# Attention and a gated FFN on one core: all 896 tokens of batches 4 and 5 through Strassen units of 448 columns, and the attention's visits dealt out anew

## The chip, the core and the metric

The kernel runs on one core of a Trainium2 chip. The core has a matrix engine (TensorE, PE in the profile, with PEld for its weight loads), a vector engine (VectorE, DVE), a scalar engine (ScalarE, ACT), a general engine (GpSimd, POOL) and one that mostly issues transfers (SyncE, SP). Each engine works through its own queue of instructions in order and waits on semaphores for the others. Scores, products and sums of matmuls land in PSUM; everything else lies in SBUF.

The metric is the device time of one execution in microseconds. The times shown are medians of several runs; the profile is of one further execution, whose own time stands beside its span below. All stretches of time that are named in this document count from the first instruction of that profiled execution.

## What is computed

Eight batches of 448 tokens, twelve heads of 64. Attention without a mask gives x with 8 x 448 = 3584 rows of 768, and a gated FFN with 1536 hidden columns follows:

```python
scores = scale * (q @ k.transpose(0, 1, 3, 2))
attn = softmax(scores)
x = (attn @ v).transpose(0, 2, 1, 3).reshape(3584, 768)
g = x @ w_gate                      # 768 -> 1536
silu = g * (1.0 / (1.0 + exp(-g)))
out = (silu * (x @ w_val)) @ w_out  # 1536 -> 768
```

Inputs and output are fp32; the loads turn q, k, v and the weights to fp16, sums stay fp32.

## The kernel before

**Two streams on TensorE.** Heads are taken in pairs: 48 pairs, six for a batch. For a pair, TensorE makes the scores transposed (`qk`, `qk_quad`, rows of L356 and L368: keys on the partitions, queries along the columns), ScalarE takes the exponential of a chunk of both heads (L376, 128 x 896), TensorE multiplies by V with a column of ones for the row sums (`pv_mm`, L457), and VectorE divides (`pv_close`: a reciprocal L499 and a product L500 for each head) into `xt`. SP turns `xt` into X, the FFN's input with features on the partitions (`turn_x`, L545 and L551). The FFN works on X in blocks of tokens: two batches make 896 tokens (`kk` 0 to 3), cut into a block of 384 and one of 512 (`block`). Blocks are numbered 0 to 7; blocks 4 and 5 are the tokens of batches 4 and 5.

**A step** (`Step`) is one of the twelve slices of 128 hidden columns of a block: six matmuls for the gate (`gp`, `gate`), six for the value (`vp`, `value`), all L605. ScalarE takes a tanh of the gate (`sg`, L632), VectorE makes t = (sg + 1) gp (L660) and hts = t vp (L666), the hidden activations. A step can be cut: then the value goes in two halves of columns, the first into a spare half of the gate's PSUM tile and only the second into a buffer of its own.

**PSUM** is dealt out by two pools. `ps_s` has three tiles of two banks: each chunk of scores, each gate and the wide sums of a pair of output tiles take one. `ps_f` has two tiles of one bank: the two accumulators of P times V (one for a head), `vp` and the second sum of an output pair take them in turn. A tile is given out again when its readers are done.

**The second half of the FFN** (`w_out`) goes either plainly (`plain_out`, L700; twelve matmuls for 128 tokens and some output columns, called an output step here) or by Strassen's seven products for two tiles of 128 tokens at once (`OutPair.wide`, L724), whose sums of hidden activations VectorE makes (`h_sums`, L588 to L591).

**The first half by Strassen.** Batches 6 and 7 (`kk` = 3) and block 5 do not run as steps. Twelve units (`Unit`, L876), alternately gate and value, each treat two slices of hidden columns and two halves of the tokens at once by seven products of three matmuls, `w` columns wide: 448 for batches 6 and 7, 256 for block 5's 512 tokens. A unit needs four sums of weights (`weight_sums`, POOL, L839 to L842) and the stage needs four sums of tokens (`token_sums`, VectorE, L1059 to L1062). `order_of` orders a stage's instructions from estimated costs; it runs when the program is built. `run_wide` follows with the output pairs.

**What orders the attention.** An opening is written out by hand. After it, a plan deals out the chunks of scores, three at a time; each entry is a visit. In the program's order a visit has: its three chunks of scores, the first products of a P times V, its rest, and then what FFN work is put there. From plan entry 19 on this is read from the table VISITS, 33 entries, which I count from 0:

```python
begins, nf, ng, no, ns = VISITS[x - base]
```

`nf` is a number of steps (two run as `run_pair`, interleaved and the second cut; one as `run_single`, cut), `ng` of wide output pairs, `no` of output steps, `ns` of extra VectorE sums, and `begins` names a block whose predecessor's output work is queued. In every seventh visit (3, 10, 17, 24, 31) no P times V ends; the code calls them bare. `open_products` takes the two `ps_f` tiles of a P times V just before its first products, which go to the two heads in turn:

```python
pv_mm(pr, hx, RU, j, accs[pr][hx], j == 0, False, half if small else None)
```

The loads of q, k and v (POOL's queue, L180 and L203) run some pairs ahead; POOL copies q and k into the order that a transposing transfer needs (L240), and SP issues that transfer (`qkT`, L244). X has two buffers: batches 4 and 5 take over the one of batches 0 and 1, batches 6 and 7 the one of batches 2 and 3, whose steps must be through by then.

After the last visit come the units of block 5, with POOL's remaining weight sums, one output step, three output pairs (one of block 4, two of block 5), the units of batches 6 and 7 with a plain output of the 128 tokens left over, and three output pairs that end the kernel.

Of the kernel before, what the change touches and what calls it, by code (L numbers as in the profile page):

```python
# [17 lines left out]
NB = 2  # L18
# [5 lines left out]
RL = 4  # L24
# [41 lines left out]
def kernel(  # L66
# [898 lines left out]
    with tc.manual_schedule():  # L965
# [50 lines left out]
        def add_block(i, visits):  # L1016
            if i < B - NB - 1:
                f1, own, n = block(i)
                fvq.extend(f1)
                kk, c0, hts = own  # L1020
            else:
                own = None
# [12 lines left out]
            new = [OutPair(kk, c0, hts, t) for t in range(1 + odd)]  # L1035
# [74 lines left out]
        def run_single():  # L1110
            step = fvq.pop(0)
            step.split = step.alone = not gate_small[0]
            step.gate()
            step.value(0)
            step.finish()
            add_sum()
# [110 lines left out]
        hts5 = hview(384, 512)  # L1227
        vfree = vraw[:].rearrange("p s h c d -> p (s h c d)")
        VE = 2 * NC * D
        t5 = token_space(vfree[:, 3 * VE :], 256)  # L1230
        for x, (chunks, todo) in enumerate(plan):
# [43 lines left out]
            for _, p0 in todo:  # L1275
# [4 lines left out]
                if p0 < XPE:  # L1280
                    turns.append(p0)
                else:
# [26 lines left out]
            else:  # L1309
# [22 lines left out]
                if x == len(VISITS) + base - 6:  # L1332
                    space = raws_all[:, 0 : RL // 2].rearrange("p a t b x -> p (a t b x)")
                    wsum_space(space, 10)
# [3 lines left out]
                    wsum_space(vfree, 4)  # L1338
# [8 lines left out]
        x5 = X[KL - 1][:, :, 384:]  # L1347
# [50 lines left out]
        units = {}  # L1398
        items = unit_items(units, lambda u: Unit(u, 256, x5, t5, hts5), 256)
# [10 lines left out]
        for u in range(6, NFB):  # L1410
            items[f"W_{u}"] = (POOL_, 3.65, [f"W_{u - 1}"], lambda u=u: weight_sums(u))
        groups5 = [OutPair(KL - 1, 384, hts5, t, 1 - t) for t in range(2)]
        sums.clear()
        halves = [h_sums(hview(0, 384), 0, 0, nc.gpsimd, f0, NH // 2) for f0 in (0, NH // 2)]
        for m, fn in enumerate(fn for both in zip(*halves) for fn in both):
            items[f"G{m}"] = (POOL_, 0.95, [f"G{m - 1}" if m else f"W_{NFB - 1}"], fn)
        items["O"] = (PE_, 1.0, [f"P{n}_{NFB - 1}" for n in (2, 3, 7)], run_o)
        items[f"P4_{NFB - 1}"][2].append("O")
        run_items(items)

        def run_wide(pairs):
            for n, pair in enumerate(pairs):
                pair.wide(kept[2 * (n % 2) : 2 * (n % 2) + 2], add_sum)

        x7 = X[KL]
# [63 lines left out]
```

## Time and profile before

| what | value |
|---|---|
| median of 3 runs | 426.44 us (426.18 to 427.26) |
| the profiled execution | 426.04 us, span 424.3 us, granted TensorE clock 0.998 |
| matmuls | 4382 |
| visits 1 to 23 | 126.3 to 258.4 us |
| visits 24 to the end of the attention | 258.4 to 297.4 us |
| units of block 5, output step, three pairs | 297.4 to 347.3 us |
| units of batches 6 and 7 | 347.3 to 399.2 us |
| last three pairs and stores | 399.2 to 424.3 us |

Busy time of an engine in a stretch counts a matmul from its start to its modelled end, and matmuls overlap: "busy 99%" does not say that the next one started as early as it could. What TensorE's work takes is read from start to start in the timeline, where a row gives its start, the time to the end of its last instruction, engine, line, operation and how many instructions it merges; in brackets stands the idle time before it and who ended it.

### The profile page before, as it was taken

Reading aid. Unit: us, or ns where it says so; the run is one execution under the profiler, and the core shown is the slowest. Engines: PE = TensorE matmul, PEld = TensorE weight load, DVE = VectorE, ACT = ScalarE, POOL = GpSimd, SP = SyncE. Lnnn points to the kernel's source line nnn. Section 1 sums busy time; section 2 is a strip of 40 time slices with the busy share of each in tenths; the row PEclk is TensorE's granted clock in tenths of the full one; section 3 lists DMA queues with packets and bytes.
Section 4 is the critical chain, followed back from the end, with each engine's and each line's share of the span. In section 5 each row is a group of like instructions: output and inputs, shape, how many; then the busy total and the mean of one; then the engine's idle time right before and its main releaser. Section 6 shows DMA issues by size and latency. Waiting matters only on the chain.

```text
span 424.3 us, 10917 instructions
## 1 busy us (share of the span) xinstructions
PE 418.0 (99%) x4382; PEld 264.0 (62%) x4382; DVE 264.5 (62%) x610; ACT 243.6 (57%) x385; POOL 230.0 (54%) x351
## 2 busy tenths in 40 slices
PE   8999999999999999999999999999999999999996
PEld 3666666655556676656656766667888655555554
DVE  4767562776668564674645766577776655665662
ACT  6975667646755654655666547569655125555221
POOL 8656625997996766357448573965999000000000
PEclk9999999999999999999999999999999999999999
DMA  9999999999999999999999998831101240000124
GB/s 137 180 200 200 200 179 190 141 165 197 187 171 120 182 128 147 127 107 159 136 107 142 158 147 161 97 99 26 22 2 25 89 129 21 2 0 2 37 82 143
DMA packets 108307, 50.29 MB, mean 119 GB/s; under 512 B 60384, under 2 KB 105056, under 8 KB 108256
## 3 DMA queue, kind: packets, MB, share of 16 engines
q0 software_dynamic: 46800, 24.56, 49.2%
q1 hardware_dynamic: 61184, 24.79, 32.1%
q8 instruction: 34, 0.56, 0.6%
q10 hardware_dynamic: 272, 0.25, 0.2%
q14 instruction: 17, 0.14, 0.1%
HBM read 49.55 MB, written 11.01 MB: 143 GB/s over the span
## 4 chain that ended last, share of the span: by engine, by line
PE 95%; ACT 2%; DVE 1%; issue 1%; DVEq 0%; ACTq 0%
PE gp L605 18%; PE vp L605 12%; PE un L876 10%; PE og L724 10%; PE acc L457 8%; PE ub L876 8%; PE ob L724 8%; PE s L356 5%; PE op L700 5%; PE acc L421 2%; PE s L388 2%; PE s L368 1%; PE tp L324 1%; PE wp L166 1%; ACT E L398 1%; PE op L1070 1%
## 5 line engine op out<-in xcount | busy, mean ns | idle before, releaser
L376 ACT ACTIVATE E<-s 128x896 f16<-128x896 f32 x126 | 106.6, 918 | 50.1 <-PE s L356 35.1
L605 PE MATMUL gp<-X,wg 128*128 128x384 f16 (+1 forms) x360 | 73.1, 348 | 0.0
L240 POOL COPY qk<-qkraw 128x512 f16<-128x512 f16 x70 | 43.1, 659 | 51.6 <-DMA qkT<-qk 50.7
L605 PE MATMUL vp<-X,wv 128*128 128x384 f16 (+3 forms) x360 | 64.2, 314 | 0.0
L660 DVE SCALAR_TENSOR_TENSOR t<-sg,gp 128x384 f32<-128x384 f32 (+1 forms) x60 | 36.1, 607 | 42.3 <-ACT sg L632 42.1
L605 PEld LDWEIGHTS <-wv 128*128 128x128 f16 x492 | 46.1, 98 | 24.3
L180 POOL DMA_DIRECT2D vraw<-in_v_dram x72 | 44.0, 637 | 14.9 <-DMA wo<-in_moe_w_out_dram 7.8
L605 PEld LDWEIGHTS <-wg 128*128 128x128 f16 x360 | 32.7, 98 | 27.2 <-issue 2.2
L180 POOL DMA_DIRECT2D qkraw<-in_k_dram x70 | 42.7, 627 | 6.1 <-DMA wo<-in_moe_w_out_dram 3.9
L398 ACT ACTIVATE E<-s 112x896 f16<-112x896 f32 x48 | 40.7, 917 | 7.7 <-PE s L388 7.7
L457 PEld LDWEIGHTS <-E 128*128 128x128 f16 (+2 forms) x1224 | 38.1, 98 | 9.0 <-issue 3.2
L632 ACT ACTIVATE sg<-gp 128x384 f32<-128x384 f32 (+1 forms) x60 | 32.0, 538 | 19.3 <-PE gp L605 15.9
L457 PE MATMUL acc<-vo,E 128*128 128x65 f16 (+2 forms) x1224 | 42.2, 193 | 0.1
L724 PEld LDWEIGHTS <-hts 128*128 128x128 f16 x270 | 25.9, 98 | 16.0
L666 DVE SCALAR_TENSOR_TENSOR hts<-t,vp 128x384 f16<-128x384 f32 (+3 forms) x60 | 31.4, 523 | 5.2 <-PE vp L605 2.1
L500 DVE TENSOR_TENSOR xt<-acc,R 128x256 f16<-128x256 f32 x72 | 30.5, 424 | 2.7 <-DVE R L499 0.3
L203 POOL DMA_DIRECT2D qkraw<-in_q_dram x43 | 29.5, 686 | 4.8 <-DMA vraw<-in_v_dram 1.4
L356 PE MATMUL s<-qkT 64*64 64x448 f16 (+1 forms) x288 | 29.2, 353 | 0.4 <-DVE hts L666 0.2
L724 PE MATMUL og<-wo,hts 128*128 128x384 f16 x132 | 25.1, 326 | 0.0
L499 DVE RECIPROCAL R<-acc 128x4 f32<-128x4 f32 x72 | 12.7, 176 | 17.7 <-PE acc L457 17.7
L700 PE MATMUL op<-wo,hts 128*128 128x192 f16 (+1 forms) x168 | 21.4, 281 | 0.0
L793 ACT ACTIVATE osb<-og 128x384 f32<-128x384 f32 x11 | 5.4, 490 | 25.8 <-PE og L724 23.7
(197 smaller groups left out, 699.1 us busy)
## 6 DMA issues: line engine op xcount, KB each, us to landing
vraw<-in_v_dram POOLq DMA_DIRECT2D x72, 64.0 KB, 5.0
qkraw<-in_q_dram POOLq DMA_DIRECT2D x39, 112.0 KB, 4.6
qkraw<-in_k_dram POOLq DMA_DIRECT2D x68, 64.0 KB, 4.7
wg<-in_moe_w_gate_dram POOLq DMA_DIRECT2D x8, 288.0 KB, 10.0
wv<-in_moe_w_val_dram POOLq DMA_DIRECT2D x8, 288.0 KB, 10.6
wo<-in_moe_w_out_dram POOLq DMA_DIRECT2D x2, 1152.0 KB, 18.3
out_dram<-osb SPq DMA_DIRECT2D x7, 288.0 KB, 3.4
out_dram<-osb SPq DMA_DIRECT2D x6, 336.0 KB, 3.4
```

What stands on the lines that cost most here:

```text
L180: eng.dma_start(dst[ts(s, 64)], rows)
L240: nc.gpsimd.tensor_copy(dst.rearrange("p c h d -> p h c d"), src)
L356: nc.tensor.matmul(s[ts(half, m), hx, 0:S].rearrange("p (c q) -> p c q", q=P), lhsT=t[ts(hx, 64), ds((c + low(pr, hx)) * 128 + half * m, m ...
L376: nc.scalar.activation(e[:, 0 : 2 * S].rearrange("p (h q) -> p h q", h=2), s[:, :, 0:S], AF.Exp, scale=sm_scale)
L398: nc.scalar.activation(e[:, :, 0:S], s[0:P, :, 0:S], AF.Exp, scale=sm_scale)
L457: nc.tensor.matmul(acc[ds(lo, m), ts((j + pr % 2) % (KR + 1), D + 1)], lhsT=e[rows, ds(hx * S + j * 128 + lo, m)], rhs=Vts[pr % NV][rows, ...
L605: nc.tensor.matmul(dst[:, 0:w], lhsT=wslice(kind, self.fb, cb), rhs=X[kk][:, cb, ds(c0 + lo, w)], start=(cb == 0), stop=(cb == NCB - 1),)
L632: self.readers = [nc.scalar.activation(self.sg[:, 0:n], gp[:, 0:n], AF.Tanh, scale=0.5)]
L660: nc.vector.scalar_tensor_tensor(self.t1[:, 0:n], self.sg[:, 0:n], 1.0, self.gp[:, 0:n], ALU.add, ALU.mult)
L700: nc.tensor.matmul(op[:, 0:w], lhsT=hts[:, fb, ts(ch, 128)], rhs=wo[oh][:, fb, ds(off, w)], start=fb == 0, stop=fb == NFB - 1,)
L724: nc.tensor.matmul(dst, lhsT=lhs(n), rhs=rhs(n), start=first and n == 0, stop=n == NH - 1, skip_group_check=True)
L876: mm = nc.tensor.matmul(dst, lhsT=lhs[:, n], rhs=rhs[:, n], start=first and n == 0, stop=n == NK - 1, skip_group_check=True,)
```

## The change

Block 4's 384 tokens no longer run as steps. Batches 4 and 5 go as a whole through units of 448 columns, in the way of batches 6 and 7: the same function `units_of` now makes both stages, each with the plain output of its last 128 tokens and three output pairs. So the block of 384 and its one pair, its four output steps, the units of 256 and their two pairs go; 48 plain matmuls of 192 columns become 24 more of 384.

VISITS hands out 26 steps where it handed out 38, one to a visit mostly, and four output steps where it handed out seven, in the same 33 visits. A single step is run whole (`run_fv`) and no longer cut. Turns of X for batches 6 and 7 that come before the steps of batches 2 and 3 are through are held back and issued after the last of those steps (`held`). The token sums of batches 4 and 5 are 1344 columns wide instead of 768, lie in the raw buffers of v and of q and k, and are made in visits 28, 30, 31 and 32. POOL makes the weight sums of units 0 and 1 in visit 27, of unit 2 in visit 31 and the others in the units' stage.

```diff
         def add_block(i, visits):
-            if i < B - NB - 1:
+            if i < B - 2 * NB:
...
-            (2, 2, 0, 0, 2), (0, 2, 0, 0, 3), (0, 0, 1, 0, 0), (0, 2, 0, 0, 0), (0, 2, 0, 0, 0),
-            (0, 2, 0, 0, 0), (0, 0, 1, 0, 0), (0, 2, 0, 0, 0), (0, 2, 0, 0, 0), (3, 2, 0, 0, 1),
-            (0, 2, 0, 0, 1), (0, 0, 1, 0, 0), (0, 0, 0, 1, 0), (0, 2, 0, 0, 0), (0, 0, 0, 1, 0),
-            (0, 2, 0, 0, 0), (0, 0, 0, 1, 0), (0, 2, 0, 0, 0), (0, 0, 0, 1, 0), (0, 2, 0, 0, 0),
-            (4, 2, 0, 0, 1), (0, 2, 0, 0, 1), (0, 0, 1, 0, 0), (0, 1, 0, 0, 0), (0, 2, 0, 0, 0),
-            (0, 1, 0, 0, 0), (0, 0, 1, 0, 0), (0, 1, 0, 0, 0), (0, 2, 0, 0, 0), (0, 1, 0, 0, 0),
-            (5, 0, 0, 1, 0), (0, 0, 0, 2, 0), (0, 0, 0, 0, 0),
+            (2, 2, 0, 0, 2), (0, 1, 0, 0, 1), (0, 0, 1, 0, 0), (0, 2, 0, 0, 0), (0, 1, 0, 0, 0),
+            (0, 1, 0, 0, 0), (0, 0, 1, 0, 0), (0, 1, 0, 0, 0), (0, 1, 0, 0, 0), (0, 1, 0, 0, 0),
+            (0, 2, 0, 0, 0), (0, 1, 0, 0, 0), (0, 1, 0, 0, 0), (3, 1, 0, 0, 0), (0, 1, 0, 0, 0),
+            (0, 1, 0, 0, 0), (0, 1, 0, 0, 0), (0, 2, 0, 0, 0), (0, 1, 0, 0, 0), (0, 1, 0, 0, 0),
+            (0, 1, 0, 0, 0), (0, 1, 0, 0, 0), (0, 1, 0, 0, 0), (0, 1, 0, 0, 0), (4, 0, 1, 0, 1),
+            (0, 0, 0, 1, 1), (0, 0, 0, 1, 1), (0, 0, 1, 0, 0), (0, 0, 0, 1, 1), (0, 0, 0, 1, 1),
+            (0, 0, 0, 0, 0), (0, 0, 1, 0, 0), (0, 0, 0, 0, 0),
...
             elif n:
-                run_single()
+                run_fv()
...
+                elif fvq and fvq[0].at[0] < p0 // NHP // NB - 1:
+                    held.append(p0)
                 else:
                     turn_x(p0)
...
-            if x == len(VISITS) + base - 6:
-                tsums5 = token_sums(X[KL - 1][:, :, 384:], 256, t5)
-            if len(VISITS) + base - 6 <= x < len(VISITS) + base - 2:
-                tsums5.pop(0)()
-            for u in {len(VISITS) + base - 6: range(4), len(VISITS) + base - 2: range(4, 6)}.get(x, []):
+                    tsums6.extend(token_sums(X[KL - 1], S, t6))
+            if len(VISITS) + base - x in (5, 3, 2, 1):
+                tsums6.pop(0)()
+            for u in {len(VISITS) + base - 6: range(2), len(VISITS) + base - 2: range(2, 3)}.get(x, []):
                 weight_sums(u)
+            while held and not fvq:
+                turn_x(held.pop(0))
...
-        items = unit_items(units, lambda u: Unit(u, 256, x5, t5, hts5), 256)
+        hts = hview(0, NT)
+
+        def units_of(kk, t, last):
+            units = {}
+            items = unit_items(units, lambda u: Unit(u, S, X[kk], t, hts), S)
+            pairs = [OutPair(kk, 0, hts, p, p if last else p % 2, last and p == 2) for p in range(3)]
...
+            return items, pairs
...
+        items, pairs = units_of(KL - 1, t6, False)
...
+        run_items(items)
...
+        run_wide(pairs)
...
+        items, pairs = units_of(KL, t7, True)
         run_items(items)
```

More of the change, by code (lines that the diff above doesn't have):

```diff
@@ L1034, in add_block @@
             odd = i % 2 == 0
-            new = [OutPair(kk, c0, hts, t) for t in range(1 + odd)]
+            new = [OutPair(kk, c0, hts, t, 1 - t if i == B - 2 * NB else t) for t in range(1 + odd)]
             groups.extend(new)
@@ L1409 @@
             wsum_space(vo[:].rearrange("p h c d -> p (h c d)"), 1)
[L1410 removed]
+        wsum_space(vfree[:, 0 : 3 * VE], 4)
+        wsum_space(xts[:].rearrange("p a j d -> p (a j d)"), 8)
+        for u in range(3, NFB):
             items[f"W_{u}"] = (POOL_, 3.65, [f"W_{u - 1}"], lambda u=u: weight_sums(u))
[L1412 removed]
+        run_items(items)
+        t7 = token_space(xp.tile([128, NCB, NT], FP16, tag="X", name="T")[:].rearrange("p a b -> p (a b)"), S)
         sums.clear()
[L1414 to L1425, printed above, removed]
[L1426 to L1435 removed]
+        sums.extend(f for pair in pairs[1:] for f in pair.sums())
+        sums.extend(token_sums(X[KL], S, t7))
+        run_wide(pairs)
         Hall.append([])
@@ L1439 @@
             Hall[2].append(flat[:, 0 : NH * 128].rearrange("p (c f) -> p c f", c=NH))
[L1440 to L1454 removed]
+        items, pairs = units_of(KL, t7, True)
         run_items(items)
[L1457 to L1458 removed]
+        sums.extend(f for pair in pairs[1:] for f in pair.sums())
+        run_wide(pairs)
 _INS = ['q', 'k', 'v', 'moe_w_gate', 'moe_w_val', 'moe_w_out']
```

59 lines of the change are left out of this document (21 added, 38 removed).

## The prediction, made before the changed kernel ran

> **What bounds the kernel now.** I read the page's busy times and the chain that ended last, then the timeline, TensorE's rows first, at the places where the change puts something new.
>
> ```profile
> span 424.3 us, 10917 instructions
> PE 418.0 (99%) x4382; PEld 264.0 (62%) x4382; DVE 264.5 (62%) x610; ACT 243.6 (57%) x385; POOL 230.0 (54%) x351
> ...
> PE 95%; ACT 2%; DVE 1%; issue 1%; DVEq 0%; ACTq 0%
> ```
>
> TensorE sets the end, so what counts is its own work and every wait in front of one of its matmuls. A row's length on TensorE overlaps the next row, so I take start to start. A visit of the attention with one whole step of 384 columns (scores before it, `acc` is P times V, `gp` and `vp` the step) looks like this:
>
> ```profile
> 255.14 2.54 ACT L376 ACTIVATE E<-s 128x896 f16<-128x896 f32 x3 [0.79 <-PE s L356]
> 255.32 1.24 PE L457 MATMUL acc<-vo,E 64*128 64x65 f16 x32
> ...
> 256.40 1.14 PE L605 MATMUL gp<-X,wg 128*128 128x384 f16 x6
> ...
> 257.37 1.14 PE L605 MATMUL vp<-X,wv 128*128 128x384 f16 x6
> ...
> 257.57 0.49 ACT L632 ACTIVATE sg<-gp 128x384 f32<-128x384 f32 x1
> 258.10 0.56 DVE L660 SCALAR_TENSOR_TENSOR t<-sg,gp 128x384 f32<-128x384 f32 x1 [0.21 <-ACT sg L632]
> ...
> 258.75 0.56 DVE L666 SCALAR_TENSOR_TENSOR hts<-t,vp 128x384 f16<-128x384 f32 x1
> ```
>
> From the start of `gp` to the end of `hts`, which frees the buffer of `vp`, it is 259.31 - 256.40 = 2.91 us, though TensorE leaves the step after 1.95. For 512 columns:
>
> ```profile
> 112.07 1.46 PE L605 MATMUL gp<-X,wg 128*128 128x512 f16 x6
> ...
> 113.36 1.46 PE L605 MATMUL vp<-X,wv 128*128 128x512 f16 x6
> 113.56 0.60 ACT L632 ACTIVATE sg<-gp 128x512 f32<-128x512 f32 x1 [0.29 <-PE gp L605]
> 114.19 0.69 DVE L660 SCALAR_TENSOR_TENSOR t<-sg,gp 128x512 f32<-128x512 f32 x1 [1.01 <-ACT sg L632]
> ...
> 114.98 0.69 DVE L666 SCALAR_TENSOR_TENSOR hts<-t,vp 128x512 f16<-128x512 f32 x1
> ```
>
> Here 115.67 - 112.07 = 3.60 us against 2.59. One of the four single-step visits that the kernel now has late shows this chain holding TensorE up: the third score and the next `acc` start only as the two `hts` end (289.75 and 290.01).
>
> ```profile
> 289.39 0.35 DVE L666 SCALAR_TENSOR_TENSOR hts<-t,gp 128x192 f16<-128x192 f32 x1
> ...
> 289.66 0.35 DVE L666 SCALAR_TENSOR_TENSOR hts<-t,vp 128x192 f16<-128x192 f32 x1
> 289.80 0.37 PE L356 MATMUL s<-qkT 64*128 64x448 f16 x2 [0.20 <-DVE hts L666]
> ...
> 290.00 0.28 PE L457 MATMUL acc<-vo,E 64*128 64x65 f16 x4
> ```
>
> **The change part by part.**
>
> *TensorE's own work.* Block 4's twelve steps of 384 columns leave the visits: 12 x 1.95 = 23.4, and 15 fewer steps are cut in halves (0.50 + 0.50 against 0.97 each, 262.07 to 262.57): 23.8 us less. Four quarter outputs go (12 x 0.083 = 1.0 each) and 24 matmuls at 0.162 come: nothing. The 252 unit matmuls go from 0.1095 (297.35 to 297.68 for three) to 0.1895 (347.27 to 347.84): +20.2, the two opening ones +0.2. Net -3.4 us: the gain if nothing waits.
>
> *The wait that single steps bring.* ps_f has two buffers. A visit takes three, in order: two accumulators, then `vp`. So the second accumulator of a visit always gets the buffer of the `vp` before it, and in the changed program its first matmul, the second of P times V, waits for VectorE's `hts` of the step before. Behind it stand the rest of P times V, the gate, the value and the next scores. With two steps a visit the wait was covered: at 206.95 the scores begin, `hts` ends at 207.48, `acc` starts at 207.54. With one step, from one end of P times V to the next: 2.91 + 0.03 to the matmul + 0.95 for P times V (246.86 to 247.81) = 3.89 us with 384 columns, 3.60 + 0.03 + 0.95 = 4.58 with 512. TensorE's work in such a visit is 3.57 (254.74 to 258.44, less 0.13 by which that P times V was long) and 4.2 (0.64 scores, 0.97, 2.59). The pairs of neighbouring visits that are so bound are 7 at 384 (visits 1, 4, 5, 7, 8, 11, 12, counted from where VISITS begins) and 8 at 512 (13 to 15, 18 to 22): 7 x 0.32 + 8 x 0.38 = 5.3 us. From both sides: nothing, if an `hts` came before the scores are through; 0.45 a pair as measured at 286.03 to 290.00 (3.97) against 3.57. I take the chain's sum, since all its rows are there.
>
> *The visits, one by one*, by rows of the same kind. Up to visit 1's `acc` (126.82) both programs are the same. In visit 1 VectorE still has four closing operations until 129.96 and one more sum (0.55) ahead of `t`, so `hts` ends near 131.6 and visit 2's P times V at 132.55, 0.8 before the old one (133.33 at `og`), not the 2 that a step is worth. Group visit to next scores 6.91 (133.33 to 140.24), visit 3 to the end of 4's P times V 6.43 (to 146.67): 145.9. Two pairs of 3.89: 153.7; the group visit 8.59 (247.81 to 256.40): 162.3; two pairs: 170.0; visit 9's step, no wait since visit 10 has no P times V, 2.0, then 6.43 again: 178.5; two of 3.89: 186.2; three of 4.58 and a step: 202.6; visit 17, as 219.26 to 227.01, 7.75: 210.4; five of 4.58: 233.3; a step: visit 24 starts at 235.9 (258.44 before).
>
> *The tail, visits 24 to 33*, has no steps left. An output visit has about 2.7 us of TensorE work (2.61 to 2.80 in the four between 197 and 228) against three exponentials 0.81 apart and a copy, 2.76. Visit 24's group needs the score buffer that the first exponential frees, with no P times V beside it: 1.2 + 6.93 = 8.15. Visits 25 to 27: 13.85. Visits 28 to 31 follow ScalarE (2.76 + 2.76 + 2.43 + 0.92, then the group): 16.1, with about 1.6 of TensorE idle. The last two P times V 2.66. Together 40.8, against 38.9 before (258.44 to 297.35). VectorE's token sums, 0.85 each (the same shape at 330.4), stand ahead of the closings there; two lie under the last group, and beside POOL's sums the 768-column one took 1.27 (280.51) where it took 0.55 alone (286.03), so the last may hold the first unit's sum up by 0.15. If that cover is gone, 1 us.
>
> So the first unit starts at 276.65 instead of 297.35: -20.7.
>
> *The units of batches 4 and 5* then repeat what the last stage does with the same order: 347.27 to 399.22 = 51.95, and three wide pairs 326.79 to 347.27 = 20.48. Before, 297.35 to 347.27 = 49.92:
>
> ```profile
> 297.35 0.49 PE L876 MATMUL un<-X,wg 128*128 128x256 f16 x3
> ...
> 347.27 0.73 PE L876 MATMUL un<-X,wg 128*128 128x448 f16 x3
> ...
> 399.22 0.98 PE L724 MATMUL og<-wo,hts 128*128 128x384 f16 x5
> ```
>
> That is +22.5. POOL's weight sums (four of 0.91, 3.65 a unit) run beside units of 3.97 and start before them; late sums would cost the difference, nothing while a unit is longer.
>
> *Queues.* A pair of heads costs POOL five issues of 0.64 and two copies of 0.65, 4.5 us; six pairs in seven visits make 3.9 a visit against 4.74 on average now (5.7 before). Between 75 and 125 POOL was 90% busy and TensorE kept going, so I price this at nothing. SP gets four X transposes at once at visit 23 (1.18 each, with 1.2 to 2 for a pair's rest): about 8 us, ahead of a score transpose that is read some 20 us later.
>
> *Sum.* -20.7 + 0.15 + 22.5 = +1.95 on the profiled execution's 426.04. That execution stood 0.40 below the median of 426.44, so 428.4.
>
> *A rule that speaks against the change.* The windows over 280 to 300, where single steps already made TensorE wait, show a granted clock of 1.00. The Trainium skill, "TensorE: Matmul & The Clock Gate", section "A second HAM failure mode: psum-queue depth-cycling", says that small idle times between matmul groups that cycle through PSUM buffers can make the clock swing between half and full; the trace shows none of it; by that rule the time would be the one of rival 3.
>
> **The rivals.**
> 1. *The waits cost nothing*, because the scores take longer to issue than I count or `hts` comes earlier: 428.4 - 5.3 = 423.1, faster. For it: P times V at 115.43 and 110.99 started without a wait in single-step visits. Against it: those close one head first and need the second buffer some 0.3 later, which no visit after them does. It decides below about 0.15 a pair (3.2 us of the 5.3 must go). 14%; half of it, around 425.8, 10%.
> 2. *Transfers or POOL fall behind* at the denser pace: if POOL's waits for transposes added 15% to its 3.9 a visit, 4.5 against 3.89 in the short visits and nothing in the long ones: 7 x 0.6 = 4 us, 432. For it: POOL waited 50.7 us on score transposes; against it: those are waits of an engine that runs ahead. 14%.
> 3. *The clock drops in the waits*: the kernel's first 512-column matmuls took 0.43 against 0.216. If the step behind each of the 15 waits ran so, 7 x 1.95 + 8 x 2.59 = 34 us, 462. 2%.
>
> **How the numbers follow.** Mine holds 60%, at 426.9 to 430 of its own: the tail may be 1.5 off either way. The range reaches down into the half case and up to the POOL case. 0.3% is about what can be told from no change: 425.16 to 427.72. Faster has rival 1 and a part of its half (0.18), same the rest of it and mine's lower end (0.20), slower what is left.
>
> **What would show it.** P times V to P times V of 3.9 and 4.6 us in the single-step visits, with the second accumulator behind `hts`; visit 24 near 236, the first 448-column unit of batches 4 and 5 near 277, the last stage's near 349, and 77.0 from there to the end. It is wrong if visits of 3.6 and 4.2 appear, or if scores wait for `qkT`.

## The result, and the profile after

The changed kernel takes 428.65 us (median of 6 runs, 428.11 to 429.52) against 426.46 us for the kernel before (6 runs, 426.18 to 427.26): a ratio of 1.0049, 95% interval 1.0033 to 1.0065. It is slower by half a per cent; 428.4 had been predicted. The profiled execution of it took 429.52 us (span 427.8), the longest of the six, that of the kernel before 426.04 (span 424.3). So the two traces differ by 3.5 us where the medians differ by 2.2, and a part of what the trace shows is one execution's bad luck, to which I come back.

The page of the changed kernel, span, busy times and the chain that ended last:

```profile
span 427.8 us, 10333 instructions
PE 415.9 (97%) x4124; PEld 241.3 (56%) x4124; DVE 265.2 (62%) x575; ACT 247.3 (58%) x371; POOL 224.8 (53%) x343
...
PE 85%; DVE 7%; ACT 5%; issue 1%; DMA 1%; SPq 0%; DVEq 0%; ACTq 0%
```

TensorE is busy 2.1 us less than before (418.0), and yet the end comes later. The chain says why: it stood on TensorE for 95% of the span and now does for 85%; VectorE has gone from 1% to 7%, ScalarE from 2% to 5%. Work was taken away, and waits took its place. The table of all waits of TensorE's instructions, by line, names the largest one (total, times, longest, in us; it lists 13 of the 15 places); in the kernel before no accumulator waits for `hts`:

```profile
PE acc L457 <- DVE hts L666: 2.5, 13, 0.3
```

A visit with one step of 512 columns shows it. First TensorE's timeline, two periods of it, then VectorE's:

```profile
228.66 0.19 PE L457 MATMUL acc<-vo,E 64*128 64x65 f16 x1
229.05 1.11 PE L457 MATMUL acc<-vo,E 64*128 64x65 f16 x31 [0.20 <-DVE hts L666]
230.00 1.46 PE L605 MATMUL gp<-X,wg 128*128 128x512 f16 x6
231.30 1.46 PE L605 MATMUL vp<-X,wv 128*128 128x512 f16 x6
232.69 0.74 PE L356 MATMUL s<-qkT 64*128 64x448 f16 x6
233.27 0.19 PE L457 MATMUL acc<-vo,E 64*128 64x65 f16 x1
233.66 1.11 PE L457 MATMUL acc<-vo,E 64*128 64x65 f16 x31 [0.20 <-DVE hts L666]
```

```profile
228.31 0.69 DVE L666 SCALAR_TENSOR_TENSOR hts<-t,vp 128x512 f16<-128x512 f32 x1
...
232.13 0.69 DVE L660 SCALAR_TENSOR_TENSOR t<-sg,gp 128x512 f32<-128x512 f32 x1 [1.10 <-ACT sg L632]
232.92 0.69 DVE L666 SCALAR_TENSOR_TENSOR hts<-t,vp 128x512 f16<-128x512 f32 x1
```

The first product of P times V, into the first accumulator, starts at 233.27. The second one, into the second accumulator, starts at 233.66, 0.05 us after `hts` has ended (232.92 + 0.69 = 233.61). The timeline counts 0.20 us of idle time there, because the modelled end of the first product covers the rest; from start to start it is 0.39 us, where the two start 0.003 to 0.004 us apart in most visits of the kernel before (at 207.54 and 246.86, for instance). From one second product to the next it is 233.66 - 229.05 = 4.61 us. The same happens in all 15 pairs of visits that the prediction names: 0.32 to 0.45 us at 384 columns (7 of them, 2.5 us in all), 0.37 to 0.39 at 512 (8, 3.1 us), together 5.6 us start to start, 5.5 more than with the usual 0.004; 5.1 of it falls into the 14 pairs behind visit 3.

Below, the trace is cut into three stretches: **A**, from the first scores of visit 1 to those of visit 3; **B**, from there to the first unit of batches 4 and 5; **C**, all after it. In the changed kernel A is 14.18 us, B 138.57 and C 148.92. C is 148.9 to 149.1 in the kernels below that are made from the changed one (149.5 in one), so B reads an edit's effect on the visits apart from the scatter of A, of which more at the end. B is one execution of each kernel, though: of two pairs of kernels below whose code in B is the same, one agrees to 0.04 us (138.57 and 138.53), the other differs by 0.65 (135.11 and 135.76).

### The profile page after: what moved, and what is told of

Read it like the earlier page. It is cut to its first block, busy times and chain, and to the rows that moved or that the text cites. A ratio compares the mean times of both kernels' runs of the same rounds, so it can differ in the third digit from the quotient of the medians.

```text
span 427.8 us, 10333 instructions
## 1 busy us (share of the span) xinstructions
PE 415.9 (97%) x4124; PEld 241.3 (56%) x4124; DVE 265.2 (62%) x575; ACT 247.3 (58%) x371; POOL 224.8 (53%) x343
## 4 chain that ended last, share of the span: by engine, by line
PE 85%; DVE 7%; ACT 5%; issue 1%; DMA 1%; SPq 0%; DVEq 0%; ACTq 0%
PE gp L605 13%; PE un L876 13%; PE og L724 10%; PE ub L876 10%; PE acc L457 8%; PE ob L724 8%; PE vp L605 8%; PE op L700 4%; PE s L356 3%; ACT E L376 2%; DVE hts L666 2%; PE s L388 2%; PE acc L421 2%; DVE t L660 2%; ACT sg L632 2%; PE op L1070 2%
## 5 line engine op out<-in xcount | busy, mean ns | idle before, releaser
L605 PE MATMUL gp<-X,wg 128*128 128x384 f16 (+1 forms) x288 | 61.4, 353 | 0.0
L605 PE MATMUL vp<-X,wv 128*128 128x384 f16 (+3 forms) x288 | 58.3, 338 | 0.6 <-DVE xt L500 0.6
L240 POOL COPY qk<-qkraw 128x512 f16<-128x512 f16 x70 | 43.0, 662 | 25.6 <-DMA qkT<-qk 24.9
L660 DVE SCALAR_TENSOR_TENSOR t<-sg,gp 128x384 f32<-128x384 f32 (+1 forms) x48 | 29.5, 620 | 37.9 <-ACT sg L632 37.9
L605 PEld LDWEIGHTS <-wv 128*128 128x128 f16 x330 | 31.9, 98 | 24.7 <-DVE xt L500 1.0
L605 PEld LDWEIGHTS <-wg 128*128 128x128 f16 x288 | 25.6, 98 | 21.6 <-issue 2.0
L632 ACT ACTIVATE sg<-gp 128x384 f32<-128x384 f32 (+1 forms) x48 | 26.0, 547 | 15.7 <-PE gp L605 14.8
L666 DVE SCALAR_TENSOR_TENSOR hts<-t,vp 128x384 f16<-128x384 f32 (+3 forms) x48 | 28.0, 584 | 4.7 <-PE vp L605 1.2
L941 ACT ACTIVATE silu<-un 128x448 f32<-128x448 f32 x24 | 13.1, 544 | 21.6 <-PE un L876 19.3
L925 DVE TENSOR_TENSOR un<-ub,kept 128x448 f32<-128x448 f32 x24 | 15.1, 631 | 16.6 <-ACT kept L922 10.3
L929 DVE TENSOR_TENSOR kept<-ub,kept 128x448 f32<-128x448 f32 x24 | 15.0, 625 | 14.7 <-PE ub L876 14.7
```

The lines of the kernel that those rows point to most:

```text
L240: nc.gpsimd.tensor_copy(dst.rearrange("p c h d -> p h c d"), src)
L605: nc.tensor.matmul(dst[:, 0:w], lhsT=wslice(kind, self.fb, cb), rhs=X[kk][:, cb, ds(c0 + lo, w)], start=(cb == 0), stop=(cb == NCB - 1),)
L632: self.readers = [nc.scalar.activation(self.sg[:, 0:n], gp[:, 0:n], AF.Tanh, scale=0.5)]
L660: nc.vector.scalar_tensor_tensor(self.t1[:, 0:n], self.sg[:, 0:n], 1.0, self.gp[:, 0:n], ALU.add, ALU.mult)
L666: nc.vector.scalar_tensor_tensor(self.hts[:, self.fb, ds(lo, w)], self.t1[:, ds(lo, w)], 0.5 * HS, vp[:, 0:w], ALU.mult, ALU.mult)
```

## The experiments

The theory under test: the loss is the wait of the second accumulator for `hts`, which holds the buffer of `ps_f` that the accumulator needs. The rivals: the waits are not what costs; the shorter visits are bound by something else; the tail, which ScalarE paces, costs the time.

**Undoing parts of the change.** First, the single steps are cut in halves again, as before, in every visit that has one (a sum of VectorE's moves behind the step with it):

```diff
             elif n:
-                run_fv()
+                step = fvq.pop(0)
+                step.split = step.alone = True
+                step.gate()
+                step.value(0)
+                step.finish()
+                add_sum()
```

> The changed kernel with single steps cut in halves again as the kernel before cuts them (visits 9, 16 and 23 stay whole, as before). My theory: the chain from the gate to the last hts grows from 2.91 to 3.03 us at 384 columns (286.98 to 290.01 before) and the third score has to wait for the first half of hts, so each of the 15 links grows by about 0.1: 430.1 (429.2 to 431.0). Rival (the second accumulator does not hang on the end of hts, or a cut frees it earlier since its buffer is taken half a step later): 428.0 to 428.7 or less.

Measured: 429.47 us (428.98 to 430.96), ratio 1.0076 (1.0059 to 1.0093); B is 139.48, 0.9 more than in the changed kernel; the intervals of the two ratios overlap, so it is the trace that speaks. TensorE's timeline in the same visit:

```profile
232.98 0.55 PE L356 MATMUL s<-qkT 64*128 64x448 f16 x4
233.69 0.36 PE L356 MATMUL s<-qkT 64*128 64x448 f16 x2 [0.16 <-DVE hts L666]
233.90 1.24 PE L457 MATMUL acc<-vo,E 64*128 64x65 f16 x32
```

Most of the wait has gone from the accumulator to the third chunk of scores, since the first half of the value now sits in the gate's tile; the second accumulator's first product still comes 0.05 to 0.14 us after the first's. The period is 4.7 us. As expected: what holds TensorE is the end of `hts`, whichever buffer it sits on.

Second, the same steps dealt out two to a visit, with visits without a step between them:

```diff
-            (2, 2, 0, 0, 2), (0, 1, 0, 0, 1), (0, 0, 1, 0, 0), (0, 2, 0, 0, 0), (0, 1, 0, 0, 0),
-            (0, 1, 0, 0, 0), (0, 0, 1, 0, 0), (0, 1, 0, 0, 0), (0, 1, 0, 0, 0), (0, 1, 0, 0, 0),
+            (2, 2, 0, 0, 2), (0, 1, 0, 0, 1), (0, 0, 1, 0, 0), (0, 2, 0, 0, 0), (0, 2, 0, 0, 0),
+            (0, 0, 0, 0, 0), (0, 0, 1, 0, 0), (0, 2, 0, 0, 0), (0, 0, 0, 0, 0), (0, 1, 0, 0, 0),
...
```

> The changed kernel with its 26 steps dealt two to a visit and the visits between left without a step (visit 1 and 9 keep one). My theory: no wait for hts is left behind a pair, but a visit without a step has 1.65 us of TensorE work against 2.43 of exponentials, so a pair and an empty visit take 5.6 + 2.45 at 384 columns and 6.95 + 2.45 at 512, 0.2 more than two single visits as they ran (3.92 + 3.92, 4.6 + 4.6), more at the ends of the chains: 430 (428.7 to 432). Rival (only the single steps cost, the spread of the work is free): 423.6.

Measured: 432.28 us (431.33 to 433.39), ratio 1.0146 (1.0124 to 1.0167); B is 141.11, 2.5 more. Two visits of the timeline, the first with no step:

```profile
227.83 1.14 PE L457 MATMUL acc<-vo,E 64*64 64x65 f16 x40
228.90 0.36 PE L356 MATMUL s<-qkT 64*128 64x448 f16 x2
229.45 0.36 PE L356 MATMUL s<-qkT 64*128 64x448 f16 x2 [0.18 <-ACT E L376]
230.26 0.36 PE L356 MATMUL s<-qkT 64*128 64x448 f16 x2 [0.45 <-ACT E L376]
230.45 1.14 PE L457 MATMUL acc<-vo,E 64*128 64x65 f16 x32
231.42 2.75 PE L605 MATMUL gp<-X,wg 128*128 128x512 f16 x12
```

In B no wait for `hts` is listed any more (one of 0.3 us is left in visit 2), but behind a visit without a step the next scores come before the exponentials have freed their tiles: from the first score to the first product of P times V it is 1.55 us (228.90 to 230.45) where it is 0.58 otherwise. Two visits take 9.47 us (227.24 to 236.71) where the changed kernel takes 9.26. One step to a visit is the better dealing of the two, waits and all.

**Taking the wait away by the order of P times V.** `pv_split`, which the kernel uses in its first visits, makes head 0's twelve products first, then the eight that hold 64 rows, then head 1's. The second accumulator is then wanted 0.4 us later.

```diff
-            split = 0 <= base - x < 3
+            split = -23 <= base - x < 3
```

> The changed kernel, but in visits 1 to 23 P times V runs head by head: twelve products of the first accumulator, then the shared chunk for both, then twelve of the second. The second accumulator is then needed some 0.35 us later. My theory (the second accumulator waits for hts of the step before, 15 waits of 0.34 us on average, 5.1 in all): the waits nearly vanish, single-step visits take 3.6 and 4.25 us instead of 3.92 and 4.62, time 423.6 (423.0 to 424.6), below both kernels. Rival (the visits are long for another reason, ScalarE's pace or late transfers, and the wait only sits where it is seen): the time stays at 428.6 (427.6 to 429.2) and the waits turn up in front of the scores or the gate.

Measured: 427.48 us (426.57 to 428.91), ratio 1.0028 (1.0016 to 1.0041). Faster than the changed kernel, but by 1 us, not 5. The same edit in the kernel before, which has no such waits:

> The same edit of P times V in the same 23 visits of the kernel before. My theory: two steps a visit cover hts there, so nothing is won, 426.5 (426.0 to 427.0). Rival (head by head is the better order by itself, whatever waits): it wins what it wins in the changed kernel, some 4 to 5 us, 421.5 to 422.5.

Measured: 430.19 us (429.20 to 431.36), ratio 1.0088 (1.0069 to 1.0107): 4 us lost. So both expectations missed by 4 us, and for one reason: I had taken the order to be free. In the timeline of the changed kernel with it, the wait is gone:

```profile
229.56 0.74 PE L356 MATMUL s<-qkT 64*128 64x448 f16 x6
230.23 1.24 PE L457 MATMUL acc<-vo,E 128*128 128x65 f16 x32
231.31 1.46 PE L605 MATMUL gp<-X,wg 128*128 128x512 f16 x6
```

From the scores to P times V it is 0.67 us (0.58 in the changed kernel: 228.08 to 228.66), and P times V takes 1.08 (0.95 in the old order where nothing waits, 246.86 to 247.81 in the kernel before). Those are 0.2 us a visit. The kernel before had shown it already: its first visits, which go head by head, take 0.69 us (110.30 to 110.99) and 1.08 (110.99 to 112.07) for the same two stretches. In the records of single matmuls, a 128-row product after a 64-row one starts 92 to 95 ns later than the usual step, and a 64-row one after a 128-row one likewise: 281 ns from the last score to the first 128-row product where a 64-row product follows after 189; 121 to 125 ns between products of P times V where 29 to 39 are usual. The old order goes scores (64 rows), the eight products of 64 rows, the 24 of 128 rows, the step (128 rows): two changes a visit. Head by head makes it four. In the kernel before, 20 visits x 0.2 = 4.0 us, which is what it lost. The Trainium skill, "TensorEngine Tiling (Array Packing)", section "Key Properties", says that a change of tiling mode drains TensorE. The trace fits that and puts the delay at some 0.09 us each time.

If that is the reason, the order should be used only where there is a wait to take away.

```diff
+            split = 0 <= base - x < 3 or x - base in (2, 5, 6, 8, 9, 12, 13, 14, 15, 16, 19, 20, 21, 22, 23)
```

> The head-by-head P*V order of the experiment before, but only in the 15 visits in which the second accumulator had waited; the five other visits of 1 to 23 keep the old order. Theory: head by head adds two changes between 64-row and 128-row products to every visit (P*V start 0.09 us later after the score products, P*V 0.10 us longer), so some 0.19 to 0.20 us per visit, which the before-kernel with the same order showed as 4.0 us over 20 visits. Five visits fewer then win 0.95 us over head by head everywhere: 426.5 us (426.1 to 427.0), level with the kernel before. Rival: the loss of that order is not in the row changes but in something spread over the stage (slower exponentials or closes): no gain, 427.5 us.

Measured: 427.18 us (426.30 to 428.29), ratio 1.0012 (0.9999 to 1.0025). The ratio fell by 0.0016, 0.7 us, though the two intervals overlap and the medians are only 0.3 apart; B fell by 0.55 (136.88 to 136.33) over the four visits of it that went back to the old order, 0.14 each. Those four visits themselves (4, 7, 11 and 18) are 0.06 to 0.21 us shorter, 0.60 together. In favour of the theory, somewhat less than it said.

**Filling the wait without a change of rows.** Head 0's products of 128 rows can also go ahead of the scores, straight behind the value's matmuls, which have 128 rows too. Two changes a visit remain, and 0.36 us of work stand in the gap.

```diff
+    def pv_ahead(pr, cs):
+        pv_open(pr)
+        for c in cs:
+            pv_piece(pr, c, 0, True, False)
+        ahead0[pr] = cs
...
             for c in range(KR):
-                pv_piece(pr, c, hx)
+                if hx or c not in ahead0.get(pr, ()):
+                    pv_piece(pr, c, hx)
...
+            if x - base in LINKS:
+                for p0 in rests:
+                    pv_ahead(p0, [c for c in range(KR) if (p0, c) not in lates])
             for n, (pr, c) in enumerate(ordered if x else []):
...
                 qk(pr, c, small, late)
```

(`LINKS` holds the same 15 visits; `lates` is empty in this kernel.)

> In the 15 visits, head 0's twelve 128-row products go ahead of the visit's score products, right behind the value matmuls, which are 128-row too; so no change of rows is added, and the second accumulator's first product comes 0.36 us later after the value matmuls. Theory A (the chain tanh, gate product, hts sets the wait, and the tanh stands behind three exponentials that now start 0.36 us later): the wait shrinks from 0.39 to some 0.16 us at 512 columns and from 0.34 to 0.29 us at 384, a gain of 8 x 0.23 + 7 x 0.06 = 2.2 us, 426.4 us (425.6 to 427.2). Theory B (hts ends a fixed time after the value matmuls): the waits all go, 423.5 us.

Measured: 426.47 us (426.02 to 428.45), ratio 0.9998 (0.9985 to 1.0010): the loss is gone. The size is theory A's, but its reason holds in three visits only. TensorE's timeline in this kernel at 512 columns, and ScalarE's exponentials beside it:

```profile
229.79 0.53 PE L457 MATMUL acc<-vo,E 128*128 128x65 f16 x12
230.25 0.74 PE L356 MATMUL s<-qkT 64*128 64x448 f16 x6
230.83 0.78 PE L457 MATMUL acc<-vo,E 64*128 64x65 f16 x20
231.63 0.59 PE L617 MATMUL gp<-X,wg 128*128 128x512 f16 x2
```

```profile
230.66 2.54 ACT L376 ACTIVATE E<-s 128x896 f16<-128x896 f32 x3 [1.36 <-PE s L356]
```

The twenty products run through; the second accumulator is wanted just as `hts` has ended. But the gate's first matmul now starts 0.21 us after the last product of P times V instead of 0.03. By the order in which `ps_s` deals out its tiles it takes the one that the visit's first exponential frees, and that one, 0.92 us long, begins at 230.66 and ends near 231.58. The next wait in line stood 0.2 us behind the one removed, and the period is 4.42 us. Eleven visits of B have this late gate, 2.0 us in all. In three visits at 384 columns it is as theory A says: the tanh stands behind the exponentials, 0.27 us late, and the second accumulator still waits 0.26 us. In the kernel before, the same edit has no wait to fill:

> The kernel before with twelve products of head 0 ahead of the score products in the same visits (2, 5, 6, 8, 9, 12 to 16, 19 to 23), where it has no wait for hts to fill. Theory (the gain in the changed kernel is the filled wait and nothing else): no gain here, and a loss of up to 0.18 us in the visits in which a gate matmul then waits for the first exponential: 427.3 us (426.3 to 428.8). Rival: the order is better by itself: 424 us.

Measured: 429.44 us (428.86 to 431.34), ratio 1.0073 (1.0058 to 1.0089), worse than the range I gave: 3.0 us for 15 visits, 0.2 each. In nine of them the gate is late, 0.21 to 0.30 us from the last product and each time 0.05 us after an exponential has ended, which makes 1.9 of the 3.0 us; where the rest lies stays open. So it is not the order that wins; it is the filling of a wait.

Next, in the visit ahead of each of the 15, the third exponential goes behind the tanh of the step; where that exponential is needed by the next visit's P times V, only eight products go ahead.

```diff
+                if n == 2 and x + 1 - base in LINKS:
+                    late = True
                 qk(pr, c, small, late)
```

> As the kernel with head 0's products ahead, and in the visit before each of the 15 the third exponential is issued behind the tanh of the step instead of ahead of it (where the third exponential's pair is the next visit's, that chunk's four products stay behind the score products). Theory A (tanh queued behind the exponentials): waits fall to zero in 9 links and to about 0.12 us in 6, gain 4.3 us and 0.4 more in visit 2, 424.0 us (423.2 to 425.4), ahead of the kernel before (426.3). Theory B (tanh never waited for the exponentials): no different from the kernel without it. Rival C: the late exponentials hold back the next visit's scores or the P*V products instead, 426 us or more.

Measured: 426.26 us (425.74 to 427.03), ratio 0.9991 (0.9980 to 1.0001). B falls by 0.4 us (136.32 to 135.90), nearer to theory B than to A's 2.5. At 512 columns the tanh had not stood behind the exponentials at all: it starts 0.42 us after the gate's last matmul in both traces. It had in the three visits at 384 columns, and there the waits of 0.26 us are gone in two and 0.14 in the third. What this trace also shows is that visits with eight products ahead are shorter than those with twelve. With eight everywhere (against the kernel just told of):

```diff
-                    pv_ahead(p0, [c for c in range(KR) if (p0, c) not in lates])
+                    pv_ahead(p0, [0, 1])
```

> Eight of head 0's products ahead of the score products instead of twelve (or eight), in all 15 visits, with the third exponential behind the tanh. In the runs with twelve the wait for hts is gone but the gate matmuls begin 0.18 us late, behind the first exponential of the visit, whose score buffer they take; in the visits with eight they do not, and the period is 4.32 to 4.37 us against 4.42 to 4.45 (512 columns), 3.67 against 3.81 (384). Theory: the gate matmuls need 20 + 4 products behind the score products to find the buffer free; 4 x 0.13 and 5 x 0.08 us, 0.9 us better than 426.3: 425.4 us (425.0 to 426.0). Rival: the 0.15 us comes back as the wait for hts, no gain: 426.3 us.

Measured: 425.72 us (425.26 to 427.64), ratio 0.9988 (0.9977 to 1.0000); B is 135.11. One period of TensorE's timeline in it:

```profile
219.96 0.41 PE L464 MATMUL acc<-vo,E 128*128 128x65 f16 x8
220.29 0.38 PE L368 MATMUL s<-qkT 64*64 64x448 f16 x4
220.51 0.55 PE L356 MATMUL s<-qkT 64*64 64x448 f16 x8
220.90 1.03 PE L464 MATMUL acc<-vo,E 64*64 64x65 f16 x32
221.77 1.46 PE L624 MATMUL gp<-X,wg 128*128 128x512 f16 x6
223.06 1.46 PE L624 MATMUL vp<-X,wv 128*128 128x512 f16 x6
224.36 0.40 PE L464 MATMUL acc<-vo,E 128*128 128x65 f16 x8
```

No row carries a wait of a size that is listed (the second accumulator's first product still comes 0.13 us after the first's), and the period is 4.40 us (219.96 to 224.36) against 4.61. That is the test that counts, and it adds up. In the 14 pairs of visits in B the second accumulator's first product came 5.14 us in all after the first's; now it is 1.72, no gate is late, and B is 3.46 us shorter (138.57 to 135.11) for 3.42 us of wait less. With twelve ahead it is 0.97 us there and 2.00 of late gates, 2.17 less than 5.14, and B is 2.25 us shorter (136.32). Nothing but the place of eight small products and of one exponential was changed. In the kernel before, products ahead were tried with twelve only, where they lose; eight, and the late exponential, were not run there.

**The tail.** The prediction had the visits from 28 on paced by ScalarE. If so, half the exponential there should show it:

```diff
+        n = 1 if half_exp[0] else 2
         nc.scalar.activation(
-            e[:, 0 : 2 * S].rearrange("p (h q) -> p h q", h=2), s[:, :, 0:S], AF.Exp, scale=sm_scale
+            e[:, 0 : n * S].rearrange("p (h q) -> p h q", h=n), s[:, 0:n, 0:S], AF.Exp, scale=sm_scale
         )
...
+            half_exp[0] = x >= base + 24
```

> The changed kernel with the exponentials of visits 24 and later taken over one head's 448 columns instead of both heads' 896, so that the other head's probabilities are not computed there: ScalarE does about half of its work in the tail and nothing else changes. Theory: the visits of the tail without a step (25 to 30, 2.75 to 2.85 us each, three exponentials of 0.83 us) are paced by ScalarE, not by TensorE; the stretch from visit 24 to the first unit shrinks from 41.5 us by 1.7 to 2.1 us, 426.5 to 427.0 us. Rival: TensorE or VectorE pace the tail: no gain, 428.5 us.

Measured: 428.05 us (426.83 to 428.76), ratio 1.0029 (1.0014 to 1.0044); visit 24 to the first unit takes 40.3 us (237.51 to 277.82) against 41.5 (237.29 to 278.83). Below what theory said, and in other places. Busy time by stretches, in the changed kernel and then with half the exponentials; the first row of each is visits 25 and 26, the second 28 to 30. Behind the stretch stand its length and the busy time of PE, PEld, DVE, ACT and POOL, each with its number of instructions, then clock, DMA share and GB/s:

```profile
245.60:251.10 5.50, 5.50 (x115) 4.39 (x114) 4.87 (x14) 5.00 (x7) 2.12 (x2) 1.00 0.81 208
259.80:267.10 7.30, 7.30 (x156) 5.67 (x156) 4.67 (x15) 6.83 (x10) 0.70 (x2) 1.00 0.57 144
```

```profile
245.50:251.00 5.50, 5.50 (x117) 4.39 (x117) 4.20 (x14) 3.16 (x7) 1.89 (x2) 1.00 0.78 199
259.55:266.80 7.25, 7.25 (x153) 5.68 (x152) 4.64 (x15) 4.75 (x11) 0.75 (x2) 1.00 0.58 142
```

ScalarE's busy time falls by a third (5.00 to 3.16, 6.83 to 4.75) and the stretches stay as long, TensorE busy throughout: the visits with an output step are TensorE's. ScalarE holds TensorE only in the group visits 24 and 31, where the wide sums, and in visit 31 a chunk of scores, wait for a score tile. TensorE's timeline of the changed kernel, then with half the exponentials:

```profile
238.72 1.14 PE L724 MATMUL og<-wo,hts 128*128 128x384 f16 x6 [0.67 <-ACT E L376]
...
268.37 0.38 PE L356 MATMUL s<-qkT 64*64 64x448 f16 x4 [0.43 <-ACT E L376]
269.18 1.14 PE L724 MATMUL og<-wo,hts 128*128 128x384 f16 x6 [0.43 <-ACT E L376]
```

```profile
238.57 1.14 PE L726 MATMUL og<-wo,hts 128*128 128x384 f16 x6 [0.29 <-ACT E L377]
...
267.91 1.14 PE L726 MATMUL og<-wo,hts 128*128 128x384 f16 x6 [0.33 <-ACT E L377]
```

With half the exponentials 0.6 us are left of these 1.5, and the 0.9 that went are most of the 1.2 us.

**VectorE's sums in visits 1 and 2.** TensorE's timeline in the changed kernel shows three waits there, the first two of which the prediction did not have:

```profile
129.36 1.15 PE L605 MATMUL vp<-X,wv 128*128 128x384 f16 x6 [0.61 <-DVE xt L500]
...
131.73 0.36 PE L356 MATMUL s<-qkT 64*128 64x448 f16 x2 [0.74 <-DVE t L660]
131.94 0.19 PE L457 MATMUL acc<-vo,E 64*128 64x65 f16 x1
132.39 1.11 PE L457 MATMUL acc<-vo,E 64*128 64x65 f16 x31 [0.26 <-DVE hts L666]
```

One of the sums stood ahead of `t`, 1.45 us long where I had put 0.55. Moved behind the step:

```diff
-            (2, 2, 0, 0, 2), (0, 1, 0, 0, 1), (0, 0, 1, 0, 0), (0, 2, 0, 0, 0), (0, 1, 0, 0, 0),
+            (2, 2, 0, 0, 2), (0, 1, 0, 0, 3), (0, 0, 1, 0, 0), (0, 2, 0, 0, 0), (0, 1, 0, 0, 0),
...
+                elif x == base + 1:
+                    run_fv(True)
```

> The changed kernel with one thing moved: the sum that VectorE makes inside visit 1's step (1.45 us in the trace, ahead of the step's gate product) goes behind the step. The waits of TensorE for the gate product in visit 2 (0.74 us) and for hts (0.26 us) should go, the wait of the value matmuls for xt (0.61 us) stays, since the sums before it stay. Theory: 0.8 to 1.2 us won, 427.6 us (427.2 to 428.0). Rival: the sum is only late elsewhere (the group of visit 2 waits for it), no gain: 428.6 us.

Measured: 428.83 us (427.99 to 429.56), ratio 1.0054 (1.0041 to 1.0067): nothing won. In the trace the waits for `t` and `hts` are gone from visit 2 and A is 13.23 us instead of 14.18. But A scatters by most of that without any edit: in the kernel with half the exponentials and in the one with the steps dealt in pairs, whose code up to visit 3 is the changed kernel's, it is 13.85 and 13.51. The changed kernel's profiled execution, its longest, is at the far end of that. So the trace's 0.95 us says little, and the median says that a typical run gains nothing that can be told.

Last, eight products ahead and three sums out of the way (the lines against the changed kernel; the quiet step of visit 1 as above):

```diff
-            (2, 2, 0, 0, 2), (0, 1, 0, 0, 1), (0, 0, 1, 0, 0), (0, 2, 0, 0, 0), (0, 1, 0, 0, 0),
+            (2, 2, 0, 0, 1), (0, 1, 0, 0, 4), (0, 0, 1, 0, 0), (0, 2, 0, 0, 0), (0, 1, 0, 0, 0),
```

> As the kernel with eight products ahead; besides, the three sums that VectorE makes in visits 0 and 1 ahead of xt, of the gate product and of hts go behind the step of visit 1. Theory: the value matmuls of visit 1 no longer wait 0.90 us for xt: 0.9 us better than with eight ahead alone, 424.5 us (424.0 to 425.2), ratio to the kernel before 0.995 to 0.997. Rival: the sums are wanted by the group of visit 2, which then waits for them: no gain.

Measured: 425.41 us (423.97 to 427.82), ratio 0.9976 (0.9961 to 0.9991): the best of all here, 0.24% faster than the kernel before, the interval clear of 1, and 0.7% faster than the changed kernel. The part of the sums in it is not shown: it is 0.3 us better than eight ahead alone, where 0.9 was expected, and the two intervals overlap. The value matmuls of visit 1 still wait 0.77 us for `xt`, and in the profiled execution with eight ahead alone they did not wait for it.

| kernel | time, us | ratio to before (95%) | A | B |
|---|---|---|---|---|
| changed | 428.65 | 1.0049 (1.0033 to 1.0065) | 14.18 | 138.57 |
| steps cut | 429.47 | 1.0076 (1.0059 to 1.0093) | 13.63 | 139.48 |
| steps in pairs | 432.28 | 1.0146 (1.0124 to 1.0167) | 13.51 | 141.11 |
| head by head, all visits | 427.48 | 1.0028 (1.0016 to 1.0041) | 12.73 | 136.88 |
| head by head, 15 visits | 427.18 | 1.0012 (0.9999 to 1.0025) | 14.85 | 136.33 |
| twelve products ahead | 426.47 | 0.9998 (0.9985 to 1.0010) | 13.30 | 136.32 |
| the same, third exponential late | 426.26 | 0.9991 (0.9980 to 1.0001) | 13.33 | 135.90 |
| eight ahead, exponential late | 425.72 | 0.9988 (0.9977 to 1.0000) | 12.73 | 135.11 |
| the same, sums later | 425.41 | 0.9976 (0.9961 to 0.9991) | 13.06 | 135.76 |
| changed, half the exponentials in the tail | 428.05 | 1.0029 (1.0014 to 1.0044) | 13.85 | 137.33 |
| changed, one sum of visit 1 later | 428.83 | 1.0054 (1.0041 to 1.0067) | 13.23 | 138.53 |

(Times of different rows were taken beside different runs of the kernel before, so the ratios compare better than the times.)

## Why the prediction was right

The time, the sign and the mechanism came out as forecast: 428.4 against 428.65. Step by step:

- *The wait that single steps bring*: 5.3 us predicted for 15 pairs of visits, 5.5 measured, each at the place and by the chain that was named. The periods are 3.91 to 3.96 us at 384 columns (3.89 predicted) and 4.60 to 4.65 at 512 (4.58). That it is the cause, and not only the place where a wait is seen, the runs with products ahead showed: as soon as other work stands in the gap, 3.4 of the 5.1 us that fall into B are gone and B is 3.5 us shorter.
- *TensorE's own work*, net -3.4 us: the 252 unit matmuls did what they should, and what the fewer steps save was not measured by itself. From the first unit of batches 4 and 5 to the first of the last stage it is 72.58 us (278.83 to 351.41), and 72.43 + 0.15 was the sum. The last stage and its pairs took 76.3 against 77.0.
- *The visits, one by one*: visit 24 was put at 235.9 and starts at 237.29. Some 0.8 of that is visits 1 and 2, whose P times V ended at 133.34 instead of 132.55. There the failed step is "one more sum (0.55) ahead of `t`": it measured 1.45 in this execution. The other 0.6 is 0.04 us a visit on average, by which the periods exceed those of the sum.
- *The tail*: 41.5 us against 40.8. The sum was near, its reason half wrong. "Visits 28 to 31 follow ScalarE" does not hold for visits 28 to 30, which are bound by TensorE's work; ScalarE's part is the 1.5 us of waits in the two group visits.
- *The sum* was +1.95 us on the profiled execution. There it is +3.5: 1.4 missed up to visit 24, 0.7 in the tail, 0.6 gained at the end. The medians differ by 2.2 only, since the profiled execution of the changed kernel was 0.9 above its median and that of the kernel before 0.4 below. That the median came out 0.25 us from the forecast is better than the terms deserve.
- *Rival 1*, waits that cost nothing, is excluded by the rows above. *Rival 2*, POOL and its transfers: POOL's copies waited 24.9 us for transposes where they had waited 50.7, and no score of the visits waited for `qkT`; it did not happen. *Rival 3*, a clock that drops in the waits: with fifteen waits of 0.3 to 0.45 us the granted clock of the span was 0.999; it did not happen. The Trainium skill, "TensorE: Matmul & The Clock Gate", section "A second HAM failure mode: psum-queue depth-cycling", has the clock swing when TensorE idles shortly and often between groups that cycle through PSUM; this trace does not show it at this size and distance of waits.

With the gap filled and the sums moved, the change is faster than the kernel before by 1.0 of the 3.4 us that TensorE's own work had promised. The place of eight small products and of one exponential took the ratio from 1.0049 to 0.9988, whose interval still ends at 1. Whether the kernel before would gain from the late exponential or the moved sums was not tried.

## What to carry to other kernels

Where a change takes work off the bounding engine, look for what that work was covering: here the second step of a visit hid a chain of tanh, gate product and value product that held a PSUM buffer 0.9 us beyond the last matmul, and 5.5 us of waits ate the saving of 3.4. Such a gap is better filled with products that are ready anyway than closed by another order; and when it is filled, look for the next wait right behind it, which here was 0.2 us away.

## What the runs showed of the hardware that I had not expected

**A change between 64-row and 128-row products costs TensorE some 0.09 us.** It made a reordering of P times V that looked harmless cost 0.2 us a visit, 4.0 us in the kernel before. It is paid in both directions, and orders of products should be judged by how often they change.

**VectorE's fp16 sums of SBUF operands often stretch beside POOL's copies.** The same 768-column sum takes 0.55 us alone. The changed kernel's visit 1, VectorE and POOL:

```profile
129.77 1.45 DVE L589 TENSOR_TENSOR hts<-hts 128x768 f16<-128x768 f16 x1
```

```profile
129.54 1.25 POOL L240 COPY qk<-qkraw 128x512 f16<-128x512 f16 x2
```

In the kernel with head by head order the same sum meets only POOL's DMA issues, and takes 0.55:

```profile
129.28 0.55 DVE L589 TENSOR_TENSOR hts<-hts 128x768 f16<-128x768 f16 x1
```

```profile
128.32 1.27 POOL L180 DMA_DIRECT2D vraw<-in_v_dram  x2
```

It is not confined to visit 1. In the best kernel's profiled execution a sum met the copies at 191.4 and took 1.93 us; `t`, `hts` and TensorE came late behind it, and one visit took 5.02 us instead of 4.4:

```profile
191.20 1.93 DVE L609 TENSOR_TENSOR hsum<-hts 128x768 f16<-128x768 f16 x1
193.05 0.67 DVE L679 SCALAR_TENSOR_TENSOR t<-sg,gp 128x512 f32<-128x512 f32 x1
```

```profile
191.41 1.30 POOL L240 COPY qk<-qkraw 128x512 f16<-128x512 f16 x2
```

The Trainium skill, "SBUF — State Buffer", section "Who interferes with whom", says that a VectorE instruction with two SBUF inputs contends with a GpSimd instruction that reads SBUF, because its second input comes through a read interface that the two share. These rows agree, with 0.9 to 1.4 us added. Not every meeting costs, and the copies are not the only cause: between 60 and 235 us of the 14 profiled executions, 67 of the 97 sums of this shape that overlapped a copy took more than 0.6 us, and so did 6 of the 239 that met none. One of those six is in the changed kernel, at 127.76, where a sum took 0.99 us beside POOL's DMA issues alone. How POOL's copies fall against the sums differs between profiled executions of equal code, and I take this, without a run that shows it, for the main source of the scatter in A. Whether the copies could be kept off the sums was not tried.
